# A first exponential on one zeroed column, ahead of ScalarE's other work

## The chip, the core and the metric

The kernel runs on one core of a Trainium2 chip. The metric is the device time of one execution in microseconds (us); lower is better. The engines are called as the profile calls them: PE is TensorE's matmul side and PEld its weight loads, DVE is VectorE, ACT is ScalarE, POOL is GpSimd, SP is SyncE, which here issues nearly all loads. A `q` behind a name (SPq, ACTq) marks an issue by the engine's sequencer.

## The reference, cut to what matters

```python
# chunked attention: batch 4, 8 heads, 768 positions, head size 64, 8 memory keys
for c in range(nc):                              # chunks of 32 queries, context 16 left and 8 right
    scores = scale * np.matmul(q_c, k_full.transpose(0, 1, 3, 2))
    scores = scores - np.max(scores, axis=-1, keepdims=True)
    a = np.exp(scores)
    a = a / (np.sum(a, axis=-1, keepdims=True) + 1e-09)
    out[:, :, c_start:c_end] = np.matmul(a, v_full)
# two feed-forward layers on x [3072, 512], d_ff 2048
h = x @ w_in;  r = np.maximum(h, 0.0);  g = s * (r * r) + b;  x = g @ w_out
h = x @ w_in2; g = np.maximum(h, 0.0) + alpha * np.minimum(h, 0.0); y = g @ w_out2
```

The weights are float64 in memory. The kernel turns each of them into a high and a low part, so that a product is made of three matmuls: high by low, low by high, and high by high.

## The kernel before, in words

**Tiling.** The 3072 rows of x make 24 tiles of 128 rows and 6 blocks of 512. Attention is done tile by tile. Tiles 0 to 3 stand alone at the start (`attention_alone`), tiles 4 to 7 follow with the values of one tile and the scores of the next in one step, and the others are done two at a time beside the matmuls of the first layer. For one tile the steps are: `scores` (L401, PE), `maxima` (L419, DVE), then either `shifted` (L429, DVE), `exps` (L433, ACT) and `sums` (L437, DVE), or, for the tiles of `BY_HEAD`, `negate` (L442, DVE) and `exps_by_head` (L452, ACT, eight exponentials of 128x64 with an accumulated sum), then `recips` (L457, L458, DVE), `normal` (L475, DVE), `turn` (L466, PE transposes into `pt`), `turned` (L471, ACT, `aT`), `values` (L488, PE, `px`), and `x_high`, `x_low` (L520 on ACT, L524 on DVE), which leave the high and low part of x.

**Weights.** A slot of weights arrives as `raw` (L280, SP, pieces of 256 KB) and is converted by `convert`: ACT takes a magnitude (`magnitude`, L296, ACT's function Abs), DVE clamps, shifts and joins the two words (L299, L304, L309, L314), ACT rounds to the high part (`high`, L321, a copy), and DVE subtracts it for the low part (L327). The first two slots come as two halves, `w0i`, `w0o`, `w1i`, `w1o` (input and output matrix apart).

**The feed-forward layers.** `g1` (L633) makes `ph`, ACT or DVE apply the function, `g_high` and `g_low` split the result, and `g2` (L692 in the first layer, L694 in the second) adds it into `po`. In the second layer DVE makes the function (L659, L664), and every other 128-row piece of the result is copied out by DVE (L738) and the rest by ACT (L736).

**Order.** Nothing is scheduled by a compiler. Every step is entered in a `Plan` with an engine, an estimated cost in us, a rank and what it comes after (`plan.add`). `Plan.order` simulates the engines and writes one fixed order of steps for each of them, and each engine then goes through its own list in that order: a step at the head of a list that waits for its data holds all the steps behind it. Loads of the start go through SP in the order of `FIRST_LOADS`, which begins q0 q1 w1i v0 q3 w0o q2 v2 w0i v1 w1o q4 (a `q` step loads queries and keys of a tile, a `v` step its values). The planner also models two things of PE: a clock that is half as fast when PE was idle (`Pace.WINDOW`, 3.41 us), and instructions that arrive in blocks of 256, counted from the 184th (`Pace.BLOCK`, `Pace.FIRST`). Where two steps come out equal in the planner's time, the order of a Python set of engine names decides; in the second layer this decides whether a copy L738 stands before or behind a neighbouring L659, for both programs alike.

ACT's functions are read from a table that has to be loaded once. The build puts a table load (ACT_TABLE_LOAD) ahead of ACT's first function, behind the wait for that function's data. One table holds all functions that the kernel uses, so each of the two programs has one table load.

Of the kernel before, what the change touches and what calls it, by code (L numbers as in the profile page):

```python
# [9 lines left out]
F32 = mybir.dt.float32  # L10
F32R = mybir.dt.float32r
U32 = mybir.dt.uint32
ACTF = mybir.ActivationFunctionType
# [3 lines left out]
P = 128  # L17
# [206 lines left out]
def tile_chunk_attention_two_ffn(ctx: ExitStack, tc: tile.TileContext, qt, kw, vw, win, wout, cst, out):  # L224
    nc = tc.nc
    const = ctx.enter_context(tc.tile_pool(name="const", bufs=1))
# [13 lines left out]
    plan = Plan({"ph": 2, "g": 2, "gg": 3, "ao": 2})  # L240
# [511 lines left out]

    id_ = plan.add("POOL", 0.6, -1000, lambda: make_identity(nc, ident))
    cs = plan.add("ACT", 0.1, -1000, consts)

    for i in range(TPB):
        attention_alone(i, TILE_RANKS[i])
# [247 lines left out]
```

## Time and profile before

| what | before |
|---|---|
| median of 3 runs | 1143.71 us (1139.6 to 1144.55) |
| the profiled execution: its time, its span | 1143.53 us, 1141.8 us |
| around the span | 1.73 us |
| PE busy | 1114.9 us, 98% of the span |
| DVE, ACT busy | 605.6 us (53%), 350.8 us (31%) |
| DMA in the first two fortieths of the span | 348 and 345 GB/s, mean of the span 86 |

A row of the timeline reads: start in us from the beginning of the span, duration in us, engine, line, operation, written tile `<-` read tile, size, count, and in brackets the idle time of the engine just before it with what ended it. `<-issue` means that the engine waited for nothing that the profile shows. A row of stretches reads: the stretch, its length, busy us of each engine with the count of instructions, the granted clock of PE (1.00 is full), the share of the DMA engines' time, and GB/s.

### The profile page before, as it was taken

The page shows a single profiled execution, that of the slowest core. Times are in us where ns is not written, and L with a number is a line of the kernel's source. Part 1 is how long each engine was busy: PE and PEld are TensorE (multiplying, and loading weights), DVE is VectorE, ACT ScalarE, POOL GpSimd, SP SyncE. Part 2 cuts the span into 40 slices and gives each one's busy share as a digit, 9 for nine tenths or more (in the row PEclk, how much of TensorE's full clock was granted, in tenths as well). Part 3 has the DMA queues.
Part 4 walks back from the last instruction along what each step waited for, and adds up shares of the span by engine and source line. Part 5 has one row for each costly group of instructions (what it writes and reads, how often), then busy time and mean ns, then how long its engine had stood idle before and what let it go on. Part 6 is the DMA issues. An engine that isn't in the chain of part 4 may idle for free.

```text
span 1141.8 us, 18302 instructions
## 1 busy us (share of the span) xinstructions
PE 1114.9 (98%) x7848; PEld 925.2 (81%) x7848; DVE 605.6 (53%) x938; ACT 350.8 (31%) x615; POOL 28.8 (3%) x58
## 2 busy tenths in 40 slices
PE   4799999999999999999999999999999999999998
PEld 4788888888888888888888788888888888888886
DVE  6797935445445355434799744334334434344432
ACT  5675644432232223224564311111111111111111
POOL 0000000000000000000000000000000000000000
PEclk9899999999999999999999999999999999999999
DMA  9918121324112213005557103002002002000000
GB/s 348 345 44 303 59 80 66 130 73 148 38 65 92 83 46 112 1 1 189 180 197 251 69 1 111 1 1 102 10 1 92 19 1 91 21 1 2 37 1 37
DMA packets 46241, 98.32 MB, mean 86 GB/s; under 512 B 4944, under 2 KB 4944, under 8 KB 46160
## 3 DMA queue, kind: packets, MB, share of 16 engines
q1 hardware_dynamic: 40320, 77.22, 19.4%
q0 software_dynamic: 5696, 19.93, 4.5%
q8 instruction: 61, 1.00, 0.4%
q14 instruction: 20, 0.16, 0.1%
q10 hardware_dynamic: 144, 0.01, 0.0%
HBM read 76.16 MB, written 20.97 MB: 85 GB/s over the span
## 4 chain that ended last, share of the span: by engine, by line
PE 52%; issue 42%; DMA 3%; DVE 1%; POOL 1%; ACT 1%; SPq 0%; POOLq 0%; ACTq 0%; DVEq 0%
PE ph L633 25%; PE po L694 23%; PE po L692 3%; DMA raw<-in_wout_dram 2%; POOL x1d L731 1%; DMA kv<-in_kw_dram 1%; DMA raw<-in_win_dram 0%; PE sp L488 0%; DVE a L309 0%; DVE a L314 0%; DMA x1d<-o 0%; PE sp L401 0%; DVE gl L677 0%; PE sc L401 0%; PE turns L466 0%
## 5 line engine op out<-in xcount | busy, mean ns | idle before, releaser
L633 PE MATMUL ph<-xh,w 128*128 128x512 f32 (+1 forms) x1560 | 508.4, 388 | 1.1 <-issue 1.1
L633 PEld LDWEIGHTS ph<-xh,w 128*128 128x128 f32 x1560 | 293.4, 189 | 60.9 <-issue 1.4
L633 PE MATMUL ph<-xl,w 128*128 128x512 f32 (+1 forms) x780 | 301.8, 387 | 0.0
L672 ACT ACTIVATE gh<-g 128x512 fp32r<-128x512 f32 (+1 forms) x195 | 121.8, 625 | 462.9 <-DVE g L664 380.4
L692 PE MATMUL po<-gh,w 128*128 128x512 f32 (+1 forms) x792 | 257.5, 387 | 0.1
L694 PE MATMUL po<-w,gh 128*128 128x512 f32 x768 | 251.6, 389 | 1.0 <-DVE o L728 1.0
L677 DVE TENSOR_TENSOR gl<-g,gh 128x512 fp32r<-128x512 f32 (+1 forms) x195 | 133.0, 682 | 106.5 <-ACT gh L672 106.0
L659 DVE TENSOR_SCALAR g<-ph,cst_sb 128x512 f32<-128x512 f32 x96 | 72.0, 750 | 206.6 <-PE ph L633 206.5
L692 PEld LDWEIGHTS po<-gh,w 128*128 128x128 f32 x792 | 148.6, 189 | 30.3 <-DVE o L728 0.7
L633 PEld LDWEIGHTS ph<-xl,w 128*128 128x128 f32 x780 | 147.5, 189 | 29.1
L694 PEld LDWEIGHTS po<-w,gh 128*128 128x128 f32 x768 | 144.1, 188 | 31.6 <-DVE o L728 1.8
L692 PE MATMUL po<-gl,w 128*128 128x512 f32 (+1 forms) x396 | 152.0, 384 | 0.0
L694 PE MATMUL po<-w,gl 128*128 128x512 f32 x384 | 149.4, 389 | 0.0
L644 ACT ACTIVATE g<-ph 128x512 f32<-128x512 f32 (+1 forms) x99 | 57.9, 585 | 156.4 <-PE ph L633 155.1
L651 DVE TENSOR_TENSOR g<-g 128x512 f32<-128x512 f32 x48 | 33.2, 692 | 111.6 <-ACT g L644 111.6
L692 PEld LDWEIGHTS po<-gl,w 128*128 128x128 f32 x396 | 74.9, 189 | 14.2
L694 PEld LDWEIGHTS po<-w,gl 128*128 128x128 f32 x384 | 72.1, 188 | 15.0
L655 DVE TENSOR_SCALAR g<-g,cst_sb 128x512 f32<-128x512 f32 (+1 forms) x99 | 52.9, 534 | 45.1 <-ACT g L649 43.5
L664 DVE SCALAR_TENSOR_TENSOR g<-ph,g 128x512 f32<-128x512 f32 x96 | 66.3, 691 | 3.1
L321 ACT ACTIVATE w<-a 128x1024 fp32r<-128x1024 f32 (+1 forms) x36 | 34.8, 967 | 34.8 <-DVE a L314 33.6
L296 ACT ACTIVATE a<-raw 128x1024 f32<-128x1024 f32 (+1 forms) x36 | 37.6, 1044 | 22.2 <-DVE w L327 13.7
L327 DVE TENSOR_TENSOR w<-a,w 128x1024 fp32r<-128x1024 f32 (+1 forms) x36 | 39.5, 1100 | 3.0 <-ACT w L321 3.0
(81 smaller groups left out, 506.2 us busy)
## 6 DMA issues: line engine op xcount, KB each, us to landing
raw<-in_win_dram SPq DMA_DIRECT2D x64, 256.0 KB, 4.8
raw<-in_wout_dram SPq DMA_DIRECT2D x64, 256.0 KB, 5.2
x1d<-o POOLq DMA_DIRECT2D x24, 512.0 KB, 3.6
vd<-in_vw_dram SPq DMA_DIRECT2D x40, 256.0 KB, 5.6
kd<-in_kw_dram SPq DMA_DIRECT2D x20, 368.0 KB, 4.9
xh<-x1d SPq DMA_DIRECT2D x6, 1024.0 KB, 5.6
xl<-x1d SPq DMA_DIRECT2D x6, 1024.0 KB, 7.7
qT<-in_qt_dram SPq DMA_DIRECT2D x20, 256.0 KB, 4.2
```

The lines of the kernel that those rows point to most:

```text
L296: nc.scalar.activation(out=temp["a"], in_=words(1).bitcast(F32), func=ACTF.Abs)
L321: nc.scalar.activation(out=w[:, :, 0, :], in_=temp["a"], func=ACTF.Copy)
L327: nc.vector.tensor_sub(out=w[:, :, 1, :], in0=temp["a"], in1=w[:, :, 0, :].bitcast(F32))
L633: nc.tensor.matmul(p, lhsT=w[:, a, kk * P:(kk + 1) * P], rhs=x[:, kk, cols], start=(i == 0), stop=(i == 3 * KD - 1))
L644: nc.scalar.activation(out=new_g(u), in_=ph.pop(u), func=ACTF.Relu)
L655: nc.vector.tensor_scalar(out=g, in0=g, scalar1=cst_sb[:, 0:1], scalar2=cst_sb[:, 1:2], op0=ALU.mult, op1=ALU.add)
L659: nc.vector.tensor_scalar(out=new_g(u), in0=ph[u], scalar1=0.0, scalar2=cst_sb[:, 2 + f:3 + f], op0=ALU.min, op1=ALU.mult)
L664: nc.vector.scalar_tensor_tensor(out=g, in0=ph.pop(u), scalar=0.0, in1=g, op0=ALU.max, op1=ALU.add)
L672: nc.scalar.activation(out=gh, in_=gt[u], func=ACTF.Copy)
L677: nc.vector.tensor_sub(out=gl, in0=gt.pop(u), in1=gh.bitcast(F32))
L692: nc.tensor.matmul(po[d][:, cols], lhsT=w[:, a, ds_], rhs=g, start=start, stop=stop)
L694: nc.tensor.matmul(po[d], lhsT=g[:, ds_], rhs=w[:, a, :], start=start, stop=stop)
```

## The change

A column `zero` of 128x1 joins the constants. DVE sets it to 0.0, and ACT takes the exponential of it in place, as a step of rank -999 behind the load of the constants `cst_sb`. Nothing reads the column afterwards.

```diff
     id_ = plan.add("POOL", 0.6, -1000, lambda: make_identity(nc, ident))
     cs = plan.add("ACT", 0.1, -1000, consts)
+    zero = const.tile([P, 1], F32, name="zero")
+
+    def first_exp():
+
+        nc.scalar.activation(out=zero, in_=zero, func=ACTF.Exp)
+
+    zd = plan.add("DVE", 0.1, -1000, lambda: nc.vector.memset(zero, 0.0))
+    plan.add("ACT", 1.7, -999, first_exp, [zd])
```

ACT's instructions at the start of the program, before (`a<-raw` is the magnitude of a weight, `e` the exponential of a tile, `aT` its transposed copy):

```order
L751 DMA cst_sb<-in_cst_dram 128x18
L296 ACT_TABLE_LOAD
L296 ACTIVATE a<-raw 128x512
L433 ACTIVATE e<-e 128x512
L452 ACTIVATE e,rs<-sc,nm 128x64 x6
L296 ACTIVATE a<-raw 128x512
L471 ACTIVATE aT<-pt 128x512
```

And with the change:

```order
L751 DMA cst_sb<-in_cst_dram 128x18
L759 ACT_TABLE_LOAD
L759 ACTIVATE zero<-zero 128x1
L296 ACTIVATE a<-raw 128x512
L433 ACTIVATE e<-e 128x512
L452 ACTIVATE e,rs<-sc,nm 128x64 x6
L296 ACTIVATE a<-raw 128x512
```

The table load now belongs to the new exponential and stands ahead of the wait for the first weight; everything behind it keeps its order.

DVE's instructions at the start, with the change (a row with + is new, the other rows stand as before):

```order
+L761 MEMSET zero 128x1
 L416 MEMSET sc 32x4x16
 L419 TENSOR_REDUCE m<-sc 128x4
```

The memset is DVE's first instruction, ahead of its first wait for PE. The orders of PE, POOL and SP are those of before.

## Prediction

> **What bounds the kernel now.** I read the page first, then the stretches, then the timelines of the first 45 us, engine by engine, since the change lies there.
>
> ```profile
> span 1141.8 us, 18302 instructions
> PE 1114.9 (98%) x7848; PEld 925.2 (81%) x7848; DVE 605.6 (53%) x938; ACT 350.8 (31%) x615; POOL 28.8 (3%) x58
> ...
> q8 instruction: 61, 1.00, 0.4%
> ...
> 0.00:8.72 8.72, 2.35 (x128) 1.92 (x128) 2.01 (x7) 0.00 (x0) 0.70 (x6) 1.00 0.77 260
> 8.72:10.02 1.30, 0.00 (x0) 0.00 (x0) 0.49 (x2) 1.28 (x2) 0.00 (x0) 1.00 1.05 398
> 10.02:20.00 9.98, 5.22 (x136) 4.31 (x136) 8.99 (x22) 7.70 (x26) 0.00 (x0) 1.00 1.05 389
> 20.00:30.00 10.00, 7.55 (x219) 6.85 (x211) 9.59 (x24) 8.04 (x38) 0.00 (x0) 1.00 1.05 383
> 30.00:40.00 10.00, 6.46 (x230) 5.62 (x233) 9.90 (x21) 7.43 (x19) 0.00 (x0) 0.94 0.83 292
> ...
> 49.02:1137.71 1088.69, 1086.86 (x7080) 1.00 0.21 75
> ```
>
> PE is the bound: from 49.02 us to its last matmul it idles 1088.69 - 1086.86 = 1.83 us (the last row has PE alone). So a gain must come from the first 43 us, where PE is idle about half of the time and where DMA is saturated from 8.72 to 30 us (share 1.05, 383 to 398 GB/s). What counts is when PE gets through these 43 us, not when ACT does.
>
> What stands in PE's way there is first the attention of tile 0, and then a chain of instruction fetches:
>
> ```profile
> 13.40 1.09 PE L466 MATMUL pt<-ident,e 128*128 128x128 f32 x4 [4.97 <-DVE e L475]
> 15.17 1.93 PE L488 MATMUL px<-aT,vd 64*64 64x32 f32 x64 [0.69 <-ACT aT L471]
> 18.81 1.33 PE L401 MATMUL sc<-kv,qa 64*32 64x64 f32 x64
> 24.98 0.92 PE L401 MATMUL sp<-kd,qT 64*32 64x64 f32 x44 [1.98 <-issue]
> 30.99 0.40 PE L633 MATMUL ph<-xh,w 128*128 128x256 f32 x2 [1.09 <-issue]
> 36.19 0.53 PE L488 MATMUL px<-qa,kv 64*64 64x32 f32 x18 [0.38 <-issue]
> 43.49 0.85 PE L488 MATMUL sp<-aT,vd 64*64 64x32 f32 x19 [2.54 <-issue]
> ```
>
> Four times PE stops inside a run of matmuls with nothing that it waits for. The 61 packets of the instruction queue hold 1.00 MB, 16.4 KB each, and PE's 7848 + 7848 instructions divided by 61 are 257: so nearly all of these packets are PE's, one for each 256 instructions. By the planner's count such a block is entered about 40 instructions into the scores at 18.81 (near 19.2 us), and then at 24.98, 30.99, 36.19 and 43.49. Each block is asked for when the one before is entered, so the steps of 5.8, 6.0, 5.2 and 7.3 us are fetches through the saturated DMA engines. PE reaches 43.49 earlier only by as much as it reaches the scores at 18.81 earlier.
>
> **The change, part by part.** What is removed from the path is the table load:
>
> ```profile
> 3.09 5.56 DMA raw<-in_win_dram
> ...
> 0.74 0.38 ACTq L751 DMA_DIRECT2D cst_sb<-in_cst_dram  x1
> 8.72 1.28 ACT L296 ACT_TABLE_LOAD   x1 [8.72 <-DMA raw<-in_win_dram]
> 10.02 0.66 ACT L296 ACTIVATE a<-raw 128x512 f32<-128x512 f32 x1
> 10.58 0.61 ACT L433 ACTIVATE e<-e 128x512 f32<-128x512 f32 x1
> ...
> 13.54 0.33 ACT L452 ACTIVATE e<-sc,nm 128x64 f32<-128x64 f32 x1
> 13.74 0.23 ACT L452 ACTIVATION_READ_ACCUMULATOR e<-sc,nm 128x1 f32 x1
> 13.83 0.70 ACT L296 ACTIVATE a<-raw 128x512 f32<-128x512 f32 x1
> 14.52 0.60 ACT L471 ACTIVATE aT<-pt 128x512 f32<-128x512 f32 x1
> ...
> 5.95 0.11 DVE L416 MEMSET sc<- 32x64 f32 x1 [5.95 <-PE sc L401]
> 10.71 0.43 DVE L299 TENSOR_SCALAR a<-a 128x512 f32<-128x512 f32 x1 [1.50 <-ACT a L296]
> ```
>
> The first row is of the chain of waits, the others are of the timelines. Today the load starts when the first weight has landed (3.09 + 5.56 = 8.65) and holds ACT for 10.02 - 8.72 = 1.30 us, and DVE with it (1.50 us of idle time at 10.71). With the change it runs from about 0.74 + 0.38 = 1.12 to 2.40 us, and the new exponential behind it. That one is not in the trace: an exponential of 128x64 takes 0.33, a read of 128x1 takes 0.23, so 0.2 to 0.3 us; I take 0.3. The memset costs the 0.11 of DVE's row. All of it is over by 2.8 us, and ACT has nothing to do until 8.72, DVE until 5.95: cost zero, with 5.9 us of cover. If that cover were gone, the price would be 1.28 + 0.3 = 1.6 us on ACT. Behind the new exponential on ACT's list waits L296, which cannot start before 8.65.
>
> So L296, the exponential L433, DVE's sums and the eight by-head exponentials of tile 1 all move 1.30 us earlier. The last of them ends at 13.97 - 1.30 = 12.67, and L296 at 13.83 could start then. It is the magnitude of the second weight half, w0o, and this is where I think the gain stops:
>
> ```profile
> 7.14 0.33 SPq L280 DMA_DIRECT2D raw<-in_wout_dram  x1
> ...
> DMA to landing us min/median/max: 6.5/6.5/6.5
> ...
> SPq L384 <- DMA raw<-in_wout_dram: 0.2, 1, 0.2
> 13.61 0.33 SPq L384 DMA_DIRECT2D vd<-in_vw_dram  x1
> ```
>
> The second piece of w0o is issued at 7.14 and lands 6.5 us later, about 13.6; SP's next issue, which is released by that landing, goes out at 13.61. This time doesn't move with ACT: SP waits for landings only here, and DMA is full. A function starts about 0.07 us after its data (8.65 to 8.72 in the first case). So L296 goes from 13.83 to 13.68: of 1.30 us there remain **0.15 us**, and 1.0 us becomes idle time of ACT.
>
> The copy `aT` at 14.52 stands behind it in ACT's list. Its data, the transposes of 13.40, would be there 1.3 us earlier, but ACT takes it at 14.37. `values` go from 15.17 to 15.02, the scores of 18.81 to 18.66, the entry into the fetched block by the same 0.15, and so 24.98 becomes 24.83 and 43.49 becomes 43.34. DVE's first step on w0o waits for the same magnitude, and so also moves by 0.15. Later landings at which ACT waits already don't move either, and can only take from it.
>
> What 0.15 us at 43.34 is worth depends on the clock:
>
> ```profile
> 35.37:38.78 3.41, 1.27 (x83) 1.00 0.59 211
> 38.78:42.19 3.41, 2.17 (x99) 0.50 0.86 263
> ...
> 43.49:49.02 5.53, 5.53 (x41) 0.50 1.04 385
> ```
>
> PE comes back at half clock and keeps it until 49.02. The changes at 38.78 and 49.02 are 10.24 us apart, three times 3.41. If the point of return stays where it is, 0.15 us earlier at half clock is worth 0.08; if it moves along, 0.15. I take 0.1. The sum: 1143.53 - 0.1 = **1143.4 us**, against a profiled execution that is 0.18 below the median of 1143.71. The bounds of the unknown are 0 (the second landing comes 0.15 later) and 1.30 us (it isn't the limit), and on the side of loss the clock, below.
>
> **The rivals.** *A, all of the 1.30 us comes through* (chance 0.11). For it: the 1.50 us of DVE and the 4.97 us for which PE waits for tile 0 both lie behind the table load, and DVE is 90 to 99% busy afterwards, so that an early start could be kept. Against it: the landing at 13.6 and ACT's fixed list. It would have to be that w0o lands 1.1 us earlier in most runs. PE would then be back at 42.19, the beginning of a 3.41 us window, so that the clock could return at 45.61 in place of 49.02. The work of 43.49 to 49.02 is worth 2.77 us at full clock; from 42.19 it would be done at 45.61 + 2.77 - 1.71 = 46.67. That is 2.35 us of gain, 1141.2 us, or 1142.2 without the clock's part.
>
> The Trainium skill (ScalarE: Activation LUTs, section "What ACT_TABLE_LOAD costs") gives 1283 ns for the load and another 1380 ns of drain, 2.66 us for a switch. By this rule A would free 2.66 us in place of 1.30 and end near 1140.9 us, an estimate by that page. The trace agrees on the load (1.28) and shows no drain behind it: the magnitude starts 0.02 us after the load ends.
>
> *B, slower: PE misses a return of its clock* (chance 0.10). The clock came up inside the run of matmuls that starts at 24.98:
>
> ```profile
> 25.13:28.54 3.41, 3.41 (x117) 1.00 1.05 383
> 28.54:31.96 3.42, 2.33 (x21) 1.00 1.05 379
> 31.96:35.37 3.41, 3.00 (x108) 1.00 1.03 376
> ...
> 27.09 0.41 PE L633 MATMUL ph<-xl,w 128*128 128x256 f32 x1
> 29.62 0.28 PE L633 MATMUL ph<-xl,w 128*128 128x256 f32 x1
> 31.22 0.28 PE L633 MATMUL ph<-xl,w 128*128 128x256 f32 x1
> ```
>
> At 27.09 a matmul of 256 columns takes 0.41 us, at 31.22 it takes 0.28 (the clock column reads 1.00 for both, since it shows no change before the first recorded one; the durations tell them apart). Of the window 25.13 to 28.54 PE was busy for all 3.41 us. That run begins only 0.15 us before the window and lasts to about 29.9. Moved 0.15 us earlier it still fills the window; moved by more than about 1.36 us, or with the windows lying otherwise against the program, it fills none, and PE stays at half clock to 38.78. The work there is 2.33 + 3.00 + 1.27 = 6.60 us, in 10.24 us. Twice that is 13.2: at least 2.96 us longer, where all idle time takes it up, at most 6.6. That gives 1146.4 to 1150.0 us. Against it: my shift is far below 1.36 us, and no row ties the windows to ACT.
>
> The Trainium skill (TensorE: Matmul & The Clock Gate, section "What's actually happening") says that the window is 4096 cycles, 3413 ns, and runs freely, without a restart with the kernel. The trace agrees on the length; that the start is free no single trace can show. By this rule B would strike some executions of either program.
>
> *C, the change doesn't do what it says* (0.04): the table is loaded a second time ahead of L296. The order of the changed program has one load only, which speaks against it. The time would be 1143.5.
>
> The second layer's L738 and L659 may swap by a tie of the planner, in either program. DVE waits for PE before most of its L659 there and runs at 53% overall; I put nothing for it.
>
> **How the numbers follow.** My forecast, 0.75: 1143.4 us. One execution of this kernel can lie at 1139.6 and another at 1144.55, and about 0.5% (5.7 us) is what a measurement here can tell from no change. The low end is the lowest run shown less 0.15, 1139.4, which takes in A; the high end is B's lower price, 1146.5. Faster by over 0.5% means below 1138.0: neither the forecast nor A gets there, 0.03. Slower by over 0.5% means above 1149.4: the upper part of B, 0.03. No change: 0.94.
>
> **What would show it.** In the changed profile the table load stands near 1.1 us and the first L296 at 8.72. Right: ACT idles about 1 us before the second L296, put down to `raw<-in_wout_dram`, which starts near 13.7; `values` begin near 15.0, the first fetch stall ends near 24.8, and PE comes back near 43.3. A is shown by `aT` near 13.2 and PE at 42.2. B is shown by matmuls of 0.41 us between 30 and 38 us. Wrong altogether would be a shift of PE at 43.5 by more than 0.5 us while the second L296 starts at 13.7: then the chain of fetches isn't what passes the time on.

## The result, and the profile after

The changed kernel is slower. Its median is 1158.53 us (4 runs, 1155.19 to 1161.33), that of the kernel before 1144.13 us (4 runs, 1139.6 to 1144.77). The ratio is 1.0133, with a 95% interval of 1.0093 to 1.0174. The prediction was no change: 1143.4 us, in a range of 1139.4 to 1146.5. It was wrong, and the measured time lies 12 us above that range.

The page of the changed kernel, its span, its busy times and three groups of matmuls:

```profile
span 1155.1 us, 18301 instructions
PE 1130.3 (98%) x7848; PEld 923.2 (80%) x7848; DVE 604.9 (52%) x939; ACT 351.0 (30%) x616; POOL 28.7 (2%) x58
L633 PE MATMUL ph<-xh,w 128*128 128x512 f32 (+1 forms) x1560 | 517.0, 394 | 0.0
L633 PE MATMUL ph<-xl,w 128*128 128x512 f32 (+1 forms) x780 | 306.3, 393 | 0.0
L694 PE MATMUL po<-w,gh 128*128 128x512 f32 x768 | 252.5, 390 | 0.6 <-DVE o L728 0.6
```

The same groups of the page before:

```profile
L633 PE MATMUL ph<-xh,w 128*128 128x512 f32 (+1 forms) x1560 | 508.4, 388 | 1.1 <-issue 1.1
L633 PE MATMUL ph<-xl,w 128*128 128x512 f32 (+1 forms) x780 | 301.8, 387 | 0.0
L694 PE MATMUL po<-w,gh 128*128 128x512 f32 x768 | 251.6, 389 | 1.0 <-DVE o L728 1.0
```

PE is busy 15.4 us longer with the same 7848 matmuls, and DVE and ACT are not busier. The mean matmul of L633 takes 6 ns longer. The loss is not at the start: the first matmul of 512 columns comes earlier than before. Its row in the timeline of the kernel before, and then the same of the changed one:

```profile
60.42 0.40 PE L633 MATMUL ph<-xh,w 128*128 128x512 f32 x1
```

```profile
55.95 0.40 PE L633 MATMUL ph<-xh,w 128*128 128x512 f32 x1
```

From there to the end it takes 1081.3 us before and 1099.1 us after (from the spans before rounding, 1141.76 and 1155.09). These 17.8 us more, less the 4.5 us gained at the start, are the 13.3 us between the two spans. The chain of waits around 800 us, deep in the second layer, shows the pace. The columns are start, duration, and what, with the count of matmuls. Before:

```profile
800.43 2.72 PE ph L633 x12
803.15 2.72 PE po L694 x12
805.87 2.72 PE ph L633 x12
808.59 2.72 PE po L694 x12
```

After:

```profile
801.73 2.80 PE ph L633 x12
804.53 2.75 PE po L694 x12
807.28 2.80 PE ph L633 x12
810.08 2.75 PE po L694 x12
```

PE waits for nothing in either piece. Twelve matmuls of L633 take 0.08 us more, 233 in place of 227 ns each, and twelve of L694 take 0.03 more. The row of a stretch of 300 us says the same without a chain: 1326 matmuls before, 1300 after, each at full clock and with PE busy all the time (a matmul that reaches over an edge of the stretch is counted too).

```profile
700.00:1000.00 300.00, 300.00 (x1326) 1.00 0.10 38
```

```profile
700.00:1000.00 300.00, 300.00 (x1300) 1.00 0.11 43
```

300 us / 1326 is 226.2 ns, 300 us / 1300 is 230.8.

What the edit touches besides the table is memory. The built program gives each tile of 128 partitions one byte address, the same in all of them. In the program before, x (`xh`, `xl`) begins at byte 17120 of each partition, the weights at 49888 and the split results `gh` at 215520. The column takes 32 bytes between x and the weights: x stays, the weights begin at 49920, `gh` at 215552, and every other working tile moves by 32 as well.

### The profile page after: what moved, and what is told of

Its sections match the earlier page's. It is cut to its first block, busy times and chain, and to the rows that moved or that the text cites. A ratio compares the mean times of both kernels' runs of the same rounds, so it can differ in the third digit from the quotient of the medians.

```text
span 1155.1 us, 18301 instructions
## 1 busy us (share of the span) xinstructions
PE 1130.3 (98%) x7848; PEld 923.2 (80%) x7848; DVE 604.9 (52%) x939; ACT 351.0 (30%) x616; POOL 28.7 (2%) x58
## 4 chain that ended last, share of the span: by engine, by line
PE 48%; issue 42%; DMA 5%; DVE 2%; POOL 1%; ACT 1%; SPq 0%; POOLq 0%; ACTq 0%; DVEq 0%
PE ph L633 24%; PE po L694 23%; PE po L692 2%; DMA raw<-in_wout_dram 1%; DMA spill<-os 1%; POOL x1d L731 1%; DMA kd<-in_kw_dram 1%; DMA kv<-in_kw_dram 1%; DMA raw<-in_win_dram 1%; PE sp L488 0%; DVE a L309 0%; DVE gl L677 0%; DMA x1d<-o 0%; DVE a L314 0%; PE sp L401 0%
## 5 line engine op out<-in xcount | busy, mean ns | idle before, releaser
L633 PE MATMUL ph<-xh,w 128*128 128x512 f32 (+1 forms) x1560 | 517.0, 394 | 0.0
L633 PEld LDWEIGHTS ph<-xh,w 128*128 128x128 f32 x1560 | 293.0, 189 | 68.0 <-issue 0.2
L633 PE MATMUL ph<-xl,w 128*128 128x512 f32 (+1 forms) x780 | 306.3, 393 | 0.0
L692 PE MATMUL po<-gh,w 128*128 128x512 f32 (+1 forms) x792 | 257.5, 387 | 0.0
L694 PE MATMUL po<-w,gh 128*128 128x512 f32 x768 | 252.5, 390 | 0.6 <-DVE o L728 0.6
L692 PEld LDWEIGHTS po<-gh,w 128*128 128x128 f32 x792 | 148.0, 188 | 32.1 <-DVE o L728 0.3
L633 PEld LDWEIGHTS ph<-xl,w 128*128 128x128 f32 x780 | 147.1, 189 | 32.4
L694 PEld LDWEIGHTS po<-w,gh 128*128 128x128 f32 x768 | 144.3, 188 | 34.0 <-DVE o L728 1.5
L692 PE MATMUL po<-gl,w 128*128 128x512 f32 (+1 forms) x396 | 152.7, 385 | 0.0
L694 PE MATMUL po<-w,gl 128*128 128x512 f32 x384 | 150.5, 392 | 0.0
L692 PEld LDWEIGHTS po<-gl,w 128*128 128x128 f32 x396 | 74.5, 188 | 14.8
L694 PEld LDWEIGHTS po<-w,gl 128*128 128x128 f32 x384 | 71.9, 187 | 15.7
L296 ACT ACTIVATE a<-raw 128x1024 f32<-128x1024 f32 (+1 forms) x36 | 37.5, 1043 | 29.5 <-DVE w L327 13.6
```

Source lines behind the costliest of these rows:

```text
L296: nc.scalar.activation(out=temp["a"], in_=words(1).bitcast(F32), func=ACTF.Abs)
L633: nc.tensor.matmul(p, lhsT=w[:, a, kk * P:(kk + 1) * P], rhs=x[:, kk, cols], start=(i == 0), stop=(i == 3 * KD - 1))
L692: nc.tensor.matmul(po[d][:, cols], lhsT=w[:, a, ds_], rhs=g, start=start, stop=stop)
L694: nc.tensor.matmul(po[d], lhsT=g[:, ds_], rhs=w[:, a, :], start=start, stop=stop)
```

## The experiments

Two theories were set against each other. **Place**: the matmuls are slower because the operands lie differently to each other. **Table**: the early table load, or the new exponential, costs the time. Each kernel ran on one chip with the kernel before beside it. The first four left these numbers (in the last columns, the us of 12 matmuls each in the chain of waits near 800 us, and the time from the first 512-column matmul to the end of the profiled span; in kernels with an added line above them, L633 and L694 stand as L634 and L695):

| kernel | moved against before: x, weights, gh (bytes) | early table load | median, before | ratio (95%) | L633, L694 x12 | from first 512-column matmul |
|---|---|---|---|---|---|---|
| before | 0, 0, 0 | no | | | 2.72, 2.72 | 1081.3 |
| the change | 0, 32, 32 | yes | 1158.53, 1144.13 | 1.0133 (1.0093 to 1.0174) | 2.80, 2.75 | 1099.1 |
| e1_column_only | 0, 32, 32 | no | 1160.29, 1142.99 | 1.0147 (1.0125 to 1.0170) | 2.80, 2.75 | 1099.8 |
| e2_exp_64_bytes | 0, 64, 64 | yes | 1157.94, 1142.99 | 1.0136 (1.0109 to 1.0163) | 2.80, 2.74 | 1098.4 |
| e3_exp_ahead_of_x | 32, 32, 32 | yes | 1141.23, 1142.99 | 0.9984 (0.9967 to 1.0002) | 2.72, 2.72 | 1082.3 |
| e4_exp_no_shift | 0, 0, 0 | yes | 1144.20, 1142.99 | 1.0006 (0.9993 to 1.0020) | 2.72, 2.72 | 1081.4 |

**The column without the exponential** (e1), one part of the change alone:

```diff
+    zero = const.tile([P, 1], F32, name="zero")
+    plan.add("DVE", 0.1, -1000, lambda: nc.vector.memset(zero, 0.0))
```

> The column and its memset alone, without the exponential: the table is loaded behind the first weight as before, and everything that is allocated behind x (weights, converted pieces, split results) lies 32 bytes higher, as in the changed kernel. Theory 'place' (first-layer-style matmuls L633 take longer because x and the weights no longer lie alike to 64 bytes): 1157 to 1163 us, L633 start to start 232 to 235 ns as in the changed profile (227 before), no early table load. Theory 'table' (the early load or the new exponential costs the time): within 0.5% of before, L633 at 227 ns.

It is as slow as the whole change, with the table loaded where it was before. Its chain of waits and its table load:

```profile
801.17 2.80 PE ph L633 x12
803.97 2.75 PE po L694 x12
```

```profile
8.47 1.28 ACT L296 ACT_TABLE_LOAD   x1 [8.47 <-DMA raw<-in_win_dram]
```

So 32 bytes of memory, which nothing ever reads, cost 1.5%. The theory "table" falls. The memset that comes with the column is no cause either: e4 and e10 below have it too and lose nothing.

**The change without a move** (e4), the other part alone. The column is put in the padding of a tile that is there:

```diff
-    cst_sb = const.tile([P, 2 + KF], F32, name="cst_sb")
+    cst_wide = const.tile([P, 3 + KF], F32, name="cst_sb")
+    cst_sb = cst_wide[:, 0:2 + KF]
...
-    zero = const.tile([P, 1], F32, name="zero")
+    zero = cst_wide[:, 2 + KF:3 + KF]
```

> The change with the column as a 19th float behind the 18 constants of cst_sb, in the space that was padding: nothing moves, and only the memset, the early table load and the exponential are left of the change. Theory 'place': what the prediction on record was about, 1143 us or up to 4 us less, L633 at 227 ns. Theory 'table': 1155 to 1162 us.

1.0006: this is what the prediction was about, the early load with nothing moved, and it comes out as no change.

**A move by 64 bytes** (e2), and **a move of x too** (e3):

```diff
-    zero = const.tile([P, 1], F32, name="zero")
+    zero16 = const.tile([P, 16], F32, name="zero")
+    zero = zero16[:, 0:1]
```

> The change with a column of 16 floats (64 bytes) in place of 1, the exponential still on 128x1: everything behind x moves by 64 bytes. Theory 'place' with 64 bytes as the measure: 1139 to 1145 us, L633 back at 227 ns. Theory 'place' with 128 bytes as the measure, or any move at all: 1155 to 1162 us. Theory 'table': 1155 to 1162 us.

```diff
     cst_sb = const.tile([P, 2 + KF], F32, name="cst_sb")
+    zero = const.tile([P, 1], F32, name="zero")
...
-    zero = const.tile([P, 1], F32, name="zero")
```

> The change with the column allocated ahead of x, so that x and everything behind it move by 32 bytes together. Theory 'place', where only the difference of x and weights counts: 1139 to 1145 us, L633 at 227 ns. Theory 'place', where weights at a multiple of 64 bytes are slow by themselves: 1155 to 1162 us. Theory 'table': 1155 to 1162 us.

e3 keeps the pace of before. Its chain:

```profile
802.06 2.72 PE ph L634 x12
804.78 2.72 PE po L695 x12
```

With the weights at the same place as in the changed kernel (49920), but x moved along, it is 2.72 again. So that place of the weights costs nothing by itself; the distance of the two counts. e2 was a miss of my guess that the measure is 64 bytes. Four more kernels asked for the measure and for what must fit to what; all leave the exponential out, and the table is loaded as before.

| kernel | moved: x, weights, gh | median, before | ratio (95%) | L633, L694 x12 |
|---|---|---|---|---|
| e5_behind_128 | 0, 128, 128 | 1159.48, 1144.52 | 1.0147 (1.0114 to 1.0180) | 2.79, 2.73 |
| e6_behind_96 | 0, 96, 96 | 1160.60, 1144.52 | 1.0144 (1.0101 to 1.0186) | 2.81, 2.73 |
| e7_x_alone_32 | 32, 128, 128 | 1160.12, 1144.52 | 1.0141 (1.0109 to 1.0172) | 2.81, 2.73 |
| e8_split_results_32 | 0, 0, 32 | 1160.66, 1144.52 | 1.0149 (1.0121 to 1.0176) | 2.73, 2.79 |

e5 and e6 are one edit with another number of floats, 32 and 24:

```diff
+    pad = const.tile([P, 32], F32, name="pad")
+    plan.add("DVE", 0.1, -1000, lambda: nc.vector.memset(pad, 0.0))
```

> Before, with a column of 32 floats behind x and its memset, no exponential: weights and split results move by 128 bytes, x stays. Theory 'place' with a period of 128 bytes: 1139 to 1145 us, L633 at 227 ns. Rival with a period of 256 bytes or more, or 'any distance other than the one of before': 1156 to 1162 us, L633 at 231 to 235 ns.

> Before, with 24 floats (96 bytes) behind x and the memset, no exponential. Period of 128 bytes, where only an equal place within it is fast: 1156 to 1162 us, L633 at 231 to 235 ns. If what matters were a direction (weights further on than x by 32 or 64 within 128), 96 forward is 32 back and could be fast: 1139 to 1145 us.

Both lose 1.4 to 1.5%. The period of 128 bytes that I had put first after e2 falls with e5. Its chain:

```profile
801.94 2.79 PE ph L633 x12
804.73 2.73 PE po L694 x12
```

e7 puts 8 floats ahead of x and 24 behind it, so that x moves by 32 and the weights by 128:

```diff
     cst_sb = const.tile([P, 2 + KF], F32, name="cst_sb")
+    ahead = const.tile([P, 8], F32, name="ahead")
...
+    pad = const.tile([P, 24], F32, name="pad")
+    plan.add("DVE", 0.1, -1000, lambda: nc.vector.memset(pad, 0.0))
+    plan.add("DVE", 0.1, -1000, lambda: nc.vector.memset(ahead, 0.0))
```

> Before, with 32 bytes ahead of x and 96 behind it, no exponential: x moves by 32 bytes, weights and split results by 128. Theory 'place' as the relation of x to weights within 128 bytes: 1156 to 1162 us, L633 slow. Rival, the weights' own place within 128 bytes decides (they stand as before): 1139 to 1145 us, L633 at 227 ns.

It loses the same as e6, which has the same distance of x and weights (96 bytes more than before): 2.81 and 2.73 in both. The chains of e6 and of e7:

```profile
803.46 2.81 PE ph L633 x12
806.27 2.73 PE po L694 x12
```

```profile
810.61 2.81 PE ph L634 x12
813.41 2.73 PE po L695 x12
```

Since a move of 128 bytes turned out not to be neutral, e7 doesn't put the weights back in a neutral place, as its expectation assumed; it says only that equal distances give equal paces.

e8 moves the working tiles alone, `gh` and `gl` among them, which meet the weights in L692 and L694:

```diff
+    pad = work.tile([P, 8], F32, name="pad")
+    plan.add("DVE", 0.1, -1000, lambda: nc.vector.memset(pad, 0.0))
```

> Before, with 8 floats (32 bytes) between the weights and the working tiles, no exponential: x and weights stand as before, the split results gh and gl (which meet the weights in L692 and L694) move by 32 bytes. Theory 'place' as a relation of the two operands of any such matmul: L633 at 227 ns, L692 and L694 at 231 to 235 ns, so the slow lines change places, and 1156 to 1162 us. Rival, it is something of x or of L633 alone: 1139 to 1145 us.

The lines that lose change places. Its chain of waits, and its groups of L633, L692 and L694:

```profile
801.19 2.73 PE ph L633 x12
803.92 2.79 PE po L694 x12
806.72 2.73 PE ph L633 x12
809.45 2.79 PE po L694 x12
```

```profile
L633 PE MATMUL ph<-xh,w 128*128 128x512 f32 (+1 forms) x1560 | 511.9, 390 | 0.6 <-issue 0.6
L692 PE MATMUL po<-gh,w 128*128 128x512 f32 (+1 forms) x792 | 262.4, 393 | 0.0
L694 PE MATMUL po<-w,gh 128*128 128x512 f32 x768 | 256.4, 395 | 0.6 <-DVE o L728 0.6
```

L692 in the kernel before:

```profile
L692 PE MATMUL po<-gh,w 128*128 128x512 f32 (+1 forms) x792 | 257.5, 387 | 0.1
```

So it belongs to the two operands that meet in a line, whichever of them is held (loaded by PEld ahead of the matmul) and whichever streams (read during it): in L633 and L692 the weights are held, in L694 `gh` is held and the weights stream. PEld is busy for 81% of the span and PE for 98%: while one matmul streams, the held operand of a later one is already being loaded, and within a line these lie alike. So these runs don't tell whether the streamed operand must fit its own matmul's held operand or that later one's.

What would be the period then? Before, x and the first weights are 49888 - 17120 = 32768 bytes apart, a multiple of 512, and inside the tiles the operands step by multiples of 512. `gh` and the weights are 215520 - 49888 = 165632 bytes apart, 647 times 256 and no multiple of 512, and L694 runs at the same 2.72. So 256 is a candidate for the measure: the moves by 32, 64, 96 and 128 were off it. The next kernel is the change with a column of 64 floats, and beside it stand two partners that have x, weights and `gh` all moved by 32, without and with the exponential:

```diff
-    zero = const.tile([P, 1], F32, name="zero")
+    zero64 = const.tile([P, 64], F32, name="zero")
+    zero = zero64[:, 0:1]
```

> The change with a column of 64 floats (256 bytes), exponential on 128x1: weights and split results move by 256 bytes, x stays. In the kernel before, x and weights are a multiple of 512 bytes apart, gh and weights an odd multiple of 256, and both pairs take 227 ns; moves of 32, 64, 96 and 128 were slow. Theory 'place' with a period of 256 bytes: 1139 to 1145 us, L633 at 227 ns. Rival, a period of 512 or more for L633: 1155 to 1162 us.

e10 is the kernel before with 8 floats ahead of x:

```diff
     cst_sb = const.tile([P, 2 + KF], F32, name="cst_sb")
+    pad = const.tile([P, 8], F32, name="pad")
...
+    plan.add("DVE", 0.1, -1000, lambda: nc.vector.memset(pad, 0.0))
```

> Before, with 8 floats (32 bytes) ahead of x and the memset, no exponential: x, weights and split results move by 32 bytes together, the table is loaded behind the first weight. Partner of e3 and e11, which have the same places and the early table load. Theory 'place': L633 at 227 ns and the time of before. If the early load is worth its 1.3 us or more, this one is 1 to 2.5 us above e11; if the gain ends at the landing of w0o, as predicted, both are equal within 1 us; if the common move by 32 bytes is worth something by itself, both lie below before by the same.

> e3 once more, beside its partner e10: the exponential with the column ahead of x. Theory 'the gain ends at the landing of w0o': equal to e10 and to before within 1 us. Rival, the 1.30 us come through: 1 to 2.5 us below both.

| kernel | moved: x, weights, gh | early table load | median, before | ratio (95%) | L633, L694 x12 | from first 512-column matmul |
|---|---|---|---|---|---|---|
| e9_exp_256_bytes | 0, 256, 256 | yes | 1143.39, 1143.56 | 1.0000 (0.9980 to 1.0019) | 2.72, 2.72 | 1081.1 |
| e10_all_32_no_exp | 32, 32, 32 | no | 1142.65, 1143.56 | 0.9994 (0.9974 to 1.0014) | 2.72, 2.72 | 1082.1 |
| e11_exp_ahead_again | 32, 32, 32 | yes | 1143.18, 1143.56 | 0.9992 (0.9973 to 1.0010) | 2.72, 2.72 | 1082.2 |

The chain of e9, where the column is 64 times as wide as in the change:

```profile
800.09 2.72 PE ph L633 x12
802.81 2.72 PE po L694 x12
```

e9 has the pace of before with x and the weights at an odd multiple of 256 bytes, as `gh` and the weights were all along: a period of 512 falls, and so does the size of the column as a cause. And e10 and e11 (the edit of e3) answer the question of the prediction itself. With all places alike, the early table load is worth nothing that can be told: 0.9992 against 0.9994, each with an interval of 0.2% either way. The 1141.23 us of e3 was not repeated by e11, the same program.

No kernel tried is faster than the one before by more than its interval.

## Why the prediction was wrong

**The step that failed** is in "What bounds the kernel now": "from 49.02 us to its last matmul it idles 1088.69 - 1086.86 = 1.83 us", and from that, "So a gain must come from the first 43 us". That PE is the bound was right. But I went on as if its 1088.69 us from 49.02 on were a constant, and looked at the change only where it could move the start. The part-by-part account prices the memset, the table load and the exponential, and leaves out the fourth thing that the edit adds, the tile itself. It has no term; it should have been some +18 us: from the first 512-column matmul to the end it took 17.8 us more in the change, and 1099.8 - 1081.3 = 18.5 more in e1. Nothing in the trace before could have told the size, since all pairs of the feed-forward matmuls there lie at multiples of 256 bytes, and their 512-column matmuls run at one pace. But that everything allocated later moves could be read off the diff, and a bound for an unknown effect on 98% of the time belongs in the range. None of my rivals was this.

**The removed load: right in its places, its worth too small to see.** The beginning of ACT's timeline in the changed kernel:

```profile
1.18 1.28 ACT L759 ACT_TABLE_LOAD   x1 [1.18 <-PEq L997]
2.47 0.20 ACT L759 ACTIVATE zero<-zero 128x1 f32<-128x1 f32 x1
9.01 0.66 ACT L296 ACTIVATE a<-raw 128x512 f32<-128x512 f32 x1 [6.34 <-DMA raw<-in_win_dram]
...
14.68 0.66 ACT L296 ACTIVATE a<-raw 128x512 f32<-128x512 f32 x1 [1.72 <-DMA raw<-in_wout_dram]
15.24 0.58 ACT L471 ACTIVATE aT<-pt 128x512 f32<-128x512 f32 x1
```

The load was put near 1.1 us and stands at 1.18; the new exponential was taken as 0.3 and takes 0.20. The further 1380 ns of drain, which the Trainium skill (ScalarE: Activation LUTs, section "What ACT_TABLE_LOAD costs") counts with a load for every switch to a different set, don't show here either: the load ends at 2.46 and the exponential starts at 2.47. The first magnitude no longer has the load ahead of it and starts when its data is there. The second magnitude idles, for `raw<-in_wout_dram`, as forecast: that is where the 1.30 us end. The size of that idle time was off, 1.72 for 1.0, since this landing comes about 1 us later in the profiled execution than in the one before: 14.6 in place of 13.6. It swings from one execution to another: the second magnitude starts at 14.55 in e3 and at 13.39 in e11, one program. The idle time is what sets the kernels apart. In all six with the early load ACT waits for this landing, for 0.45 to 1.72 us; of the seven without it, only e1 does (0.44). Rows of e11 and of e10, which has no early load:

```profile
13.39 0.66 ACT L297 ACTIVATE a<-raw 128x512 f32<-128x512 f32 x1 [0.45 <-DMA raw<-in_wout_dram]
```

```profile
13.91 0.67 ACT L297 ACTIVATE a<-raw 128x512 f32<-128x512 f32 x1
```

So the 0.15 us of the sum is lost in the swing of the landing. Rival A, that all of the 1.30 us comes through, put the time at 1141.2 us, a ratio of 0.998, or at 0.999 without the clock's part. The interval of e4, 0.9993 to 1.0020, leaves both out; those of e9 and e11 (at 1.0000 and 0.9992) reach down to 0.9980 and 0.9973. A gain of 0.15 us (0.013%) is far below what these intervals can tell; that it is zero is not shown. One reading was off without a price: of the "eight by-head exponentials" only six stand ahead of the second magnitude, in ACT's list as in the rows, and the end taken, 13.97, is that of the sixth.

**The chain of fetches.** "`values` begin near 15.0, the first fetch stall ends near 24.8": they came at 15.88 and 25.82, later by 0.9 and 1.0, about as much as the landing was late.

```profile
15.88 1.93 PE L488 MATMUL px<-aT,vd 64*64 64x32 f32 x64 [2.40 <-ACT aT L471]
25.82 0.92 PE L401 MATMUL sp<-kd,qT 64*32 64x64 f32 x44 [2.62 <-issue]
...
41.27 0.58 PE L692 MATMUL po<-gh,w 128*128 128x256 f32 x1
```

The same step in the kernel before:

```profile
44.26 0.58 PE L692 MATMUL po<-gh,w 128*128 128x256 f32 x1
```

From there the forecast of the times did not hold. I had said that PE returns near 43.3, and that a shift by more than 0.5 us with the second magnitude near 13.7 would speak against the chain of fetches. PE began L692 at 41.27 in the changed kernel, 3 us sooner than before, although it was a microsecond late at 25.82. The other stalls that the kernel before has, at 30.99, 36.19 and 43.49, are missing here. And e10, without an early load and with its second magnitude at 13.91, ends its last stall at 42.48, 1.0 us sooner than before.

The trace's records of single DMA packets show which part of the chain holds. In the kernel before, packets of the instruction queue (16 KB each) start at 22.55, 28.64, 33.69 and 41.13 and take 0.9 to 1.2 us, and each of the four stalls ends 1.2 to 1.5 us behind the end of one of them. That fits stalls that are fetches. But the time from one packet to the next is not fixed: in the kernel before, the last of the four starts 7.4 us behind the third, and in the changed kernel 3.4 us behind it (33.87 and 37.30). In the changed kernel, e3 and e5 it starts between 36.8 and 37.5, in the other ten between 39.9 and 42.0; in the first three L692 begins by 41.3, in the others at 42.9 or later. e3 and e11, one program, stand on different sides. So PE's return differs from execution to execution by more than the change could move it, and the entry at 19.2 us does not fix it. Why the packet runs early in some executions stays open.

**The clock.** The 0.1 us that I took for 0.15 us of shift can't be tested. In the changed kernel PE was at full clock in the stretch from 43.49 to 49.02, where before it ran at half:

```profile
43.49:49.02 5.53, 5.53 (x49) 1.00 1.02 383
```

That, with the return 3 us earlier, makes up the 4.5 us by which the first 512-column matmul came sooner. e5, which has no early load, gets there as soon:

```profile
55.42 0.39 PE L633 MATMUL ph<-xh,w 128*128 128x512 f32 x1
```

And e3 and e11, one program, get there at 55.6 and 58.2. So it is a matter of the execution, and not shown to be one of the change. Rival B, half clock from 28.5 to 38.8 us, was not the cause of the loss, and C, a second table load, did not come.

**Range and chances.** 0.03 for slower by more than 0.5% was too little, and not only by bad luck: the cases that it came from were all in the first 43 us.

## What to carry to other kernels

A new tile, however small, can move all that is allocated behind it: price it by what runs on the moved tiles, and look at the built addresses before and after. In this kernel a matmul of 128x512 in float32r (the type of the high and low parts) keeps its pace where the two operands lie a multiple of 256 bytes apart. A small constant can go into padding that is there (e4) or ahead of all operands that meet in matmuls (e3, e11); behind all of them it should do no harm either, which was not run. And an engine that starts sooner gains only up to the next thing that it waits for in its fixed list: here the landing of the second weight, for which ACT then idles 0.45 to 1.72 us.

## What the runs showed of the hardware that I had not expected

The pace of these matmuls depends on the distance of their two operands in a partition. At distances that are multiples of 256 bytes (the tiles' first bytes 32768, 33024 or 165632 apart), a matmul of 128x512 float32r with its own weights starts 2.72 / 12 = 227 ns after the one before; with 32, 64, 96 or 128 bytes more it is 2.79 to 2.81 / 12 = 233 to 234 ns. The lines that are at a good distance but run between others at a bad one take 2.73 to 2.75 / 12 = 228 to 229 ns. Over the 4536 matmuls of 512 columns this comes to 17.8 us in the change and 18.5 in e1. That it is the distance, and not a place, is shown by e3 against the change (same weights' places, other x) and by e7 against e6; that both pairs have it, by e8; that 256 bytes are neutral and 128 are not, by e9 against e5. It is not so at every width: twelve matmuls of L633 with 256 columns, at full clock, take 1.42 us in the changed kernel (44.92 to 46.34) and 1.43 us before (49.32 to 50.75). Other moves between 128 and 256 bytes and other types were not tried, and what in the chip makes it so is not shown by any run here.
